# An attention layer and a feed-forward layer on one core: another order of attention steps within a pair of heads, for the first eight pairs

## The chip, the cores and the metric

The kernel runs on one core of a Trainium2 chip. The metric is the device time of one execution in microseconds (us). Five engines take part, each with a queue of its own that it works off in order: TensorE (PE, with its weight loads as PEld), VectorE (DVE), ScalarE (ACT), GpSimd (POOL), and SyncE (SP), which here only issues DMA transfers.

## The reference

A block-causal softmax attention over 8 batches of 8 heads (576 positions, head size 64), followed by a two-layer MLP with the activation h * sigmoid(1.702 h) on the 4608 rows.

```python
scores = scale * np.matmul(q, k.transpose(0, 1, 3, 2))
scores = np.where(block_i >= block_j, scores, -1e9)      # blocks of 64
scores = scores - np.max(scores, axis=-1, keepdims=True)
attn = np.exp(scores); attn = attn / (np.sum(attn, axis=-1, keepdims=True) + 1e-09)
x = np.matmul(attn, v)          # per head; then heads side by side: [4608, 512]
h = x @ w_in                    # w_in  [512, 2048]
g = h * (1.0 / (1.0 + np.exp(-1.702 * h)))
out = g @ w_out                 # w_out [2048, 512]
```

## The kernel before

Two heads form a pair; there are 32 pairs, four to a batch. The queries of a head are cut into five chunks: chunk 0 has 64 queries, chunks 1 to 4 have 128 each, and chunk i sees 64(2i+1) keys. One loop runs over the pairs n. In each turn `step(n)` calls a list of items, in the order that a string of `ORDER` gives for the phase of n: the first string for pairs 0 to 3, the second for 4 to 7, the third from pair 8 on (with `HANDOVER` in place of it for pair 8). The items are:

- a group of chunk numbers, as `1+0` or `2/3`, is `score(n, ...)`: PE multiplies queries and keys into PSUM banks, two heads at a time (a slash starts new banks); `weigh` then lets DVE read each bank, add the mask and take the maximum (line 349), and ACT take the exponential with the sum (line 356); `normalise` prepares the reciprocal on DVE (lines 366 and 369) and lets POOL scale the weights (line 374).
- `a`, `B` and `C` are `flip(...)`: PE turns the scaled weights with the identity (line 101), for chunks 0 and 1 of pair n (`a`), 2 and 3 of pair n-1 (`B`), 4 of pair n-1 (`C`); ACT copies each bank to SBUF (lines 409 and 422).
- `V` is `av(n - 1)`: PE multiplies the turned weights of pair n-1 with the values, 60 matmuls; ACT copies the sums into the ring `xr` (lines 448 and 449). Then the values of a later pair are loaded.
- `L` is `prep(n + 1)`: two DVE transpositions (line 295), first the queries, then the keys, from `raw` to `qk` of the next pair. Behind the second one the loads of a later pair's queries and keys are issued on SP (line 277, eight transfers), since `raw` has one buffer (pairs 1 and 3 have one of their own).
- `-` is an empty place.

The weights of the chunks have one home each (`es[i]`, used again by every early pair), and so has the turned form `pw`. PSUM banks are handed out in rotation by `bank()`: seven of them for pairs 0 to 3, three (`w0` to `w2`) for pairs 4 to 7, where the MLP has the others.

After each item, and after each empty place, two other jobs are advanced up to a quota that is read from the position 2 * (n + (place + 1) / places): `convert`, which turns the 64-bit weights of the MLP into pairs of 32-bit ones, piece by piece (ACT line 218; DVE lines 222, 227, 232; ACT line 241; POOL line 81), and `advance`, which emits MLP matmuls. The MLP works on tiles of 384 rows. Tile 0 can't begin before the attention of pairs 0 to 3 is complete, that is behind the `V` of pair 4; its quota runs from position 8.4 to 17 (`TILES_BY`). So in pairs 0 to 3, and in pair 4 up to its `V`, PE has attention alone, and from there on MLP work lies between the items.

PE's instructions keep the order of the program (`keep_in_program_order`). Those of DVE, ACT, POOL and SP are put in order by the framework's scheduler, by priority (earlier in the program first) and by when it takes an operand to be there. Each engine then works off its queue strictly in that order.

In the steps below 2/3(1) is the scoring of chunks 2 and 3 of pair 1, V(1) the sums of values of pair 1, qk(3) the turned queries and keys of pair 3, and so on.

Of the kernel before, what the change touches and what calls it, by code (L numbers as in the profile page):

```python
# [23 lines left out]


ORDER = (
    "1+0 - B - C - V - 2/3 - L - a - 4 -",
    "1+0 - B - C - V - 2 - 3 L a - 4 - -",
    "3+0/2+1 - - - - V - 4 - - - L -",
)  # L30

# [617 lines left out]
```

## Time and profile before

| what | us |
|---|---|
| three runs, median (lowest to highest) | 1131.25 (1130.1 to 1132.11) |
| the profiled execution, its own time | 1134.02 |
| its span, first to last instruction | 1132.2 |
| PE busy in the span | 1078.8 (95%) |
| DVE, ACT, POOL busy | 586.5, 499.4, 407.1 |
| mean granted TensorE clock | 0.983 of full speed |

The profiled execution is 2.77 us over the median of the runs. Busy time says how long an engine had an instruction in hand; where it was idle, the timeline gives the idle time just before an instruction in square brackets, with what ended it.

### The profile page before, as it was taken

How to read it: one execution, taken by the hardware profiler on the slowest of the kernel's cores; microseconds unless marked ns; L12 is line 12 of the kernel's file. 1: busy time of each engine (PE TensorE's matmuls, PEld its weight loads, DVE VectorE, ACT ScalarE, POOL GpSimd, SP SyncE). 2: the span in 40 equal slices, each digit the busy share in tenths (PEclk: the TensorE clock that was granted, in tenths of full speed). 3: DMA queues.
4: the chain of work that ended last, by engine and by line, in shares of the span. 5: the costliest groups of instructions: out<-in, count | busy, mean ns of one | idle time of the engine just before them, and what ended most of it. 6: DMA issues, size and time to landing. Idle time of an engine off the chain costs nothing. (4 is left out here: it accounts for less than half of the span.)

```text
span 1132.2 us, 20021 instructions
## 1 busy us (share of the span) xinstructions
PE 1078.8 (95%) x6960; PEld 914.1 (81%) x6960; DVE 586.5 (52%) x1856; ACT 499.4 (44%) x1321; POOL 407.1 (36%) x509
## 2 busy tenths in 40 slices
PE   4779999999999999999999999999999999999998
PEld 3567777788788888888888888888888888899997
DVE  5577777554555655654545645555555555211211
ACT  5675777533433533443433434443443443322322
POOL 4455566333333323333333333333333333222222
PEclk8878999999999999999999999999999999999999
DMA  8642642133433243243343243343343332200000
GB/s 176 176 112 58 194 107 70 45 80 84 102 85 81 67 104 66 60 113 85 78 108 82 65 96 63 72 113 78 81 101 73 70 91 50 54 28 1 28 1 29
DMA packets 219366, 91.26 MB, mean 81 GB/s; under 512 B 197760, under 2 KB 197760, under 8 KB 219264
## 3 DMA queue, kind: packets, MB, share of 16 engines
q1 hardware_dynamic: 214528, 89.38, 33.6%
q8 instruction: 55, 0.90, 0.4%
q10 hardware_dynamic: 4736, 0.59, 0.3%
q14 instruction: 47, 0.39, 0.1%
HBM read 45.09 MB, written 9.44 MB: 48 GB/s over the span
## 5 line engine op out<-in xcount | busy, mean ns | idle before, releaser
L81 POOL TENSOR_TENSOR gl<-g,gh 128x384 fp32r<-128x384 f32 x192 | 194.9, 1015 | 528.8 <-ACT gh L561 433.6
L98 PE MATMUL hp<-xh,wih 128*128 128x384 f32 x768 | 265.4, 346 | 11.6 <-DVE g L553 10.5
L553 DVE SCALAR_TENSOR_TENSOR g<-g,hp 128x384 f32<-128x384 f32 x192 | 105.5, 550 | 324.1 <-ACT g L552 322.9
L98 PE MATMUL hp<-xh,wil 128*128 128x384 f32 x768 | 259.1, 337 | 0.0
L98 PE MATMUL hp<-xl,wih 128*128 128x384 f32 x768 | 253.7, 338 | 0.4 <-DVE xl L81 0.4
L552 ACT ACTIVATE g<-hp 128x384 f32<-128x384 f32 x192 | 94.3, 491 | 340.0 <-PE hp L98 337.8
L98 PE MATMUL acc<-woh,gh 128*128 128x512 f32 x576 | 232.2, 403 | 0.0
L98 PE MATMUL acc<-wol,gh 128*128 128x512 f32 x576 | 227.9, 396 | 0.0
L98 PE MATMUL acc<-woh,gl 128*128 128x512 f32 x576 | 227.3, 395 | 0.5 <-POOL gl L81 0.5
L98 PEld LDWEIGHTS hp<-xh,wih 128*128 128x128 f32 x768 | 144.7, 188 | 36.8 <-DVE g L553 21.5
L561 ACT CAST gh<-g 128x384 fp32r<-128x384 f32 x192 | 98.5, 513 | 149.8 <-DVE g L553 149.7
L356 ACT ACTIVATE e<-e,mx 64x64 f32<-64x64 f32 (+4 forms) x240 | 132.3, 552 | 63.7 <-DVE mx L349 63.7
L374 POOL TENSOR_TENSOR e<-e,sm 64x64 f32<-64x64 f32 (+1 forms) x192 | 114.1, 614 | 108.3 <-DVE sm L369 61.5
L98 PEld LDWEIGHTS hp<-xh,wil 128*128 128x128 f32 x768 | 144.8, 189 | 6.8 <-issue 0.2
L98 PEld LDWEIGHTS hp<-xl,wih 128*128 128x128 f32 x768 | 144.1, 188 | 0.7 <-DVE xl L81 0.7
L98 PE MATMUL bank<-qk 64*128 64x320 f32 (+4 forms) x768 | 119.8, 429 | 21.6 <-DVE qk L295 20.4
L98 PEld LDWEIGHTS acc<-woh,gh 128*128 128x128 f32 x576 | 108.2, 188 | 31.8 <-issue 12.0
L98 PEld LDWEIGHTS acc<-wol,gh 128*128 128x128 f32 x576 | 108.1, 188 | 23.5
L98 PEld LDWEIGHTS acc<-woh,gl 128*128 128x128 f32 x576 | 108.3, 188 | 16.7 <-POOL gl L81 1.1
L98 PEld LDWEIGHTS bank<-qk 64*128 64x128 f32 x768 | 68.7, 196 | 62.7 <-issue 26.2
L383 DVE STREAM_TRANSPOSE turned<-e 128x384 f32<-128x384 f32 (+1 forms) x192 | 92.5, 500 | 48.1 <-POOL e L374 48.0
L349 DVE CUSTOM_DVE_ANT_0 e<-bank,mask 64x64 f32<-64x64 f32 (+4 forms) x240 | 88.3, 417 | 29.8 <-PE bank L98 26.2
(50 smaller groups left out, 968.1 us busy)
## 6 DMA issues: line engine op xcount, KB each, us to landing
turned<-turned SPq DMA_DIRECT2D x192, 80.0 KB, 2.1
turned<-turned SPq DMA_DIRECT2D x96, 112.0 KB, 2.2
raw<-in_q_dram SPq DMA_DIRECT2D x128, 72.0 KB, 2.4
out_dram<-osb SPq DMA_DIRECT2D x36, 256.0 KB, 2.2
raw<-in_k_dram SPq DMA_DIRECT2D x120, 72.0 KB, 2.4
turned<-turned SPq DMA_DIRECT2D x96, 88.0 KB, 2.1
words<-in_moe_w_in_dram SPq DMA_DIRECT2D x16, 512.0 KB, 5.6
vp<-in_v_dram SPq DMA_DIRECT2D x60, 128.0 KB, 2.3
```

The source lines that it names most:

```text
L81: eng.tensor_tensor(out=out, in0=in0, in1=in1, op=ALU.subtract)
L98: return tc.keep_in_program_order(nc.tensor.matmul(**kw))
L349: nc.vector.tensor_tensor_reduce(out=e[0:m, hd, lo:hi], in0=s, in1=mk, op0=ALU.add, op1=ALU.min, scale=-0.125, scalar=3e38 if lo == 0 else ...
L356: nc.scalar.activation(out=e[0:m, hd], in_=e[0:m, hd], func=AF.Exp, scale=-1.0, bias=mx[0:m, i, hd : hd + 1], accum_out=sm[0:m, i, hd : hd ...
L374: nc.gpsimd.tensor_tensor(out=x, in0=x, in1=sc.to_broadcast([m, width(i)]), op=ALU.mult)
L383: nc.vector.transpose(out=tw[:, :, SLOT[i] : SLOT[i] + i, hd].rearrange("p b j c -> p j b c"), in_=e[:, hd, 0 : i * P],)
L552: nc.scalar.activation(out=g, in_=hp[:, 0:tt], func=AF.Tanh, scale=1.702)
L553: nc.vector.scalar_tensor_tensor(out=g, in0=g, scalar=1.0, in1=hp[:, 0:tt], op0=ALU.add, op1=ALU.mult)
L561: nc.scalar.copy(out=gh, in_=g)
```

## The change

Two strings are replaced. In pairs 0 to 3 the places go from 16 to 14, in pairs 4 to 7 from 17 to 16. In both, chunks 2 and 3 (of this pair) and `L` come ahead of `V`, and in pairs 0 to 3 chunk 4 does too; `a` comes last but for an empty place, or last but for chunk 4. In pairs 4 to 7 chunk 4 stays behind `V` and `a`. The sum of items is the same, and so are all instructions.

```diff
 ORDER = (
-    "1+0 - B - C - V - 2/3 - L - a - 4 -",
-    "1+0 - B - C - V - 2 - 3 L a - 4 - -",
+    "1+0 - B 2/3 - L C - 4 - V - a -",
+    "1+0 - B - 2 - C - 3 L V - a - 4 -",
     "3+0/2+1 - - - - V - 4 - - - L -",
 )
```

## Rows read from the trace of the kernel before

**Rows 1.** The page's part 2, busy tenths of PE in 40 slices of 28.3 us.

```profile
...
PE   4779999999999999999999999999999999999998
...
```

**Rows 2.** Windows by stage: length; busy us of PE, PEld, DVE, ACT, POOL; clock; DMA.

```profile
...
0.00:86.00 86.00, 55.90 (x465) 43.76 (x466) 53.33 (x186) 52.65 (x156) 41.95 (x65) 0.82 0.64 158
86.00:232.00 146.00, 135.91 (x883) 108.09 (x884) 103.43 (x290) 92.53 (x239) 80.48 (x87) 0.98 0.35 92
232.00:1132.00 900.00, 886.99 (x5617) 762.25 (x5613) 429.72 (x1384) 354.23 (x927) 284.71 (x357) 1.00 0.31 71
...
```

**Rows 3.** Waits of PE, 0 to 86 us: us in total, times, longest.

```profile
...
PE bank L98 <- DVE qk L295: 20.4, 4, 7.2
PE bank L101 <- POOL turned L374: 7.3, 4, 3.9
...
```

**Rows 4.** Timeline of PE: start, us, operation, [idle before it, what ended that].

```profile
...
15.03 1.79 PE L101 MATMUL bank<-ident,turned 128*128 128x128 f32 x6 [3.88 <-POOL turned L374]
...
24.91 0.33 PE L101 MATMUL bank<-ident,turned 128*128 128x128 f32 x1 [2.15 <-POOL turned L374]
...
32.99 1.56 PE L98 MATMUL bank<-qk 64*128 64x320 f32 x8
...
35.29 1.24 PE L98 MATMUL bank<-qk 64*128 64x256 f32 x8
39.30 1.33 PE L98 MATMUL bank<-qk 64*128 64x192 f32 x8 [2.77 <-DVE qk L295]
...
44.24 2.98 PE L98 MATMUL bank<-turned,vx 128*64 128x128 f32 x60
...
48.64 0.87 PE L101 MATMUL bank<-ident,turned 128*128 128x128 f32 x6
...
55.76 1.33 PE L98 MATMUL bank<-qk 64*128 64x192 f32 x8 [5.07 <-DVE qk L295]
...
62.34 2.21 PE L98 MATMUL bank<-turned,vp 128*64 128x64 f32 x44 [0.36 <-ACT turned L422]
...
74.19 1.33 PE L98 MATMUL bank<-qk 64*128 64x192 f32 x8 [5.44 <-DVE qk L295]
...
85.78 0.44 PE L98 MATMUL hp<-xh,wih 128*128 128x384 f32 x1
...
```

**Rows 5.** Timeline of DVE, the same columns, 18 to 55 us.

```profile
...
18.01 0.42 DVE L349 CUSTOM_DVE_ANT_0 turned<-bank,mask 128x256 f32<-128x256 f32 x1 [1.88 <-PE bank L98]
...
26.19 0.78 DVE L295 STREAM_TRANSPOSE qk<-raw 128x576 f32<-128x576 f32 x1
33.83 0.49 DVE L349 CUSTOM_DVE_ANT_0 turned<-bank,mask 128x320 f32<-128x320 f32 x1 [6.86 <-PE bank L98]
...
38.48 0.77 DVE L295 STREAM_TRANSPOSE qk<-raw 128x576 f32<-128x576 f32 x1
...
54.92 0.78 DVE L295 STREAM_TRANSPOSE qk<-raw 128x576 f32<-128x576 f32 x1
...
```

**Rows 6.** Timeline of POOL, around the scaling of chunk 3 of pair 0.

```profile
...
19.67 1.83 POOL L374 TENSOR_TENSOR turned<-turned,sm 128x448 f32<-128x448 f32 x2 [2.00 <-DVE sm L369]
...
```

**Rows 7.** Timeline of PE in pairs 5 and 6, where MLP work lies between.

```profile
...
114.74 0.62 PE L101 MATMUL bank<-ident,turned 128*64 128x128 f32 x4 [1.41 <-ACT turned L409]
...
142.32 1.28 PE L101 MATMUL bank<-ident,turned 128*128 128x128 f32 x10 [1.13 <-DVE mx L349]
...
```

**Rows 8.** Lines of DVE, 0 to 86 us: busy, mean ns, idle before.

```profile
...
L222 DVE TENSOR_SCALAR wm<-wm 128x512 uint32<-128x512 uint32 x9 | 6.2, 693 | 6.7 <-ACT wm L218 6.7
...
```

**Rows 9.** Source line 366, 0 to 86 us: duration ns min/median/max, first and last start.

```profile
...
L366 DVE TENSOR_SCALAR sm<-sm x22: 118/170/947, 13.0 to 79.9; 128x2 f32<-128x2 f32 x17, 64x2 f32<-64x2 f32 x5
...
```

**Rows 10.** Windows, the columns of rows 2: tile 0 begins; DVE at its busiest.

```profile
...
90.00:98.00 8.00, 7.14 (x22) 5.70 (x23) 3.95 (x9) 3.58 (x8) 4.01 (x4) 0.57 0.00 0
160.00:170.00 10.00, 9.90 (x55) 7.78 (x54) 8.26 (x31) 7.69 (x20) 6.35 (x7) 1.00 0.57 125
...
```

**Rows 11.** Timeline of SP's queue: the loads that the second transposition sets off.

```profile
...
39.27 1.96 SPq L277 DMA_DIRECT2D raw<-in_q_dram  x4
...
```

## The prediction

> **What bounds the kernel now.** I read the slices of the page first, then the windows of three stages, the waits of PE in the first stage, and last the timelines there. The slices show PE at 9 tenths nearly everywhere but in the first three [rows 1]. By the windows PE is busy 887.0 of 900 us behind 232 us and 135.9 of 146 us between 86 and 232 us, but 55.9 of the first 86 us; no other engine reaches 72% of any stage [rows 2]. So the end is set by PE, and whatever PE loses before tile 0 of the MLP begins, at 85.78 us [rows 4], moves the end one for one: behind it PE has always something to do. The first stage is where the change acts, and there PE idles 30.1 us: 20.4 us in four waits for qk, 7.3 us in four waits for weights that POOL scales [rows 3], the rest in small ones. The first qk wait, 7.2 us, is the first load; the change can't touch it. That leaves 13.3 us, which the timeline shows ahead of 1+0 of pairs 2, 3 and 4: 2.77, 5.07 and 5.44 us [rows 4]. No transfer causes them. DVE turned the queries of pair 2 at 26.19 us, then stood idle 6.86 us for the scores of chunk 2 of pair 1, and turned the keys only at 38.48 us, behind the weighing of chunks 2 to 4 of pair 1 [rows 5]. The scores it waited for stood behind V(0) on PE. DVE waits for PE and then PE for DVE, in turn: that is the loop that the change cuts.
>
> **The change part by part.** No instruction is added or removed; only places are.
>
> *Pairs 0 to 3, the qk waits.* Now, between the last score of chunk 4 of pair n and 1+0 of pair n+1, PE has nothing (2.77 to 5.44 us, above). Afterwards V(n-1) and a(n) stand there, 2.98 and 0.87 us at full clock [rows 4], 3.85 us together. DVE's way from the scores of chunk 4 to the turned keys stays as it is, since `L` was ahead of chunk 4 before too, and yet the keys come out behind chunk 4's weighing; I take that the scheduler puts them there again. Then the gaps shrink by 2.77, 3.85 and 3.85: 10.5 us. Bounds: if the keys are now turned ahead of chunk 4, all of 13.3 us; if one merge of a weight piece (three DVE instructions of 0.69 us [rows 8], 2.1 us) gets in ahead of them in each pair, 10.5 - 3 x 2.1 = 4.2 us. I take 10.5, since rows 5 show the order itself.
>
> *Pair 0, the waits for scaled weights.* a(0) waits 3.88 us for POOL [rows 4]. Chunk 4 of pair 0 now comes behind a(0) and goes ahead of it: its 1.24 us (by the same item of pair 1 [rows 4]) fill part of that wait. DVE stood 1.88 us for just these scores [rows 5], and POOL's scaling of chunk 3 started 2.00 us late on a reciprocal queued behind them [rows 6]; with that gone the two short waits in B(0), 1.3 us of the 7.3 less 3.88 and 2.15, go too. The 2.15 us wait in C(0) [rows 4] gets chunks 2 and 3 of pair 1 ahead of it, 1.56 us [rows 4]. Together 1.24 + 1.3 + 1.56 = 4.1 us; bounds 0 (POOL is what is late) and 7.3 (all POOL waits). I take 4.1, as each part has a row.
>
> *V moved behind chunk 4: queues.* V(n-1) needs ACT's copies of the turned chunk 4. On ACT these may now stand behind the exponentials of chunks 2 and 3, while only chunk 4's scores lie between C and V on PE. The nearest row is a V that waited 0.36 us for such a copy [rows 4]; three times that is 1.1 us. Bounds 0 and 3 x 1.41 = 4.2 us, the longest wait for a copy [rows 7]. On SP the transfers of a later pair's queries and keys, the four for the queries taking 1.96 us to issue [rows 11], now come ahead of the values instead of behind them. They wait for the second transposition, and the values queue behind them for that long; who needs the values is the V a whole pair on, over 13 us. I cost this at nothing; without that cover it would be 4 us or so a pair, two such groups of transfers. `prep` moved ahead of C on DVE only puts 1.5 us where DVE stood idle [rows 5].
>
> *Pair 4 up to V(3).* Tile 0 waits for V(3), and there 2(4) and 3(4) now come ahead of it, with three banks and no MLP work between. Their own PE time isn't lost: it is work that need not be done later. But three changes of bank owner (2 to C, C to 3, 3 to V) stand uncovered. Each costs between nothing and 1.41 us, the waits of such kind that show [rows 7]; I take 1.2, near the two rows, as nothing covers them: 3.6 us, bounds 0 and 4.2.
>
> *Pairs 5 to 7.* There MLP work lies between all items. Two changes from scores to another owner (2 to C, 3 to V) stand in place of one (3 to `a`). I take 0.5 us a pair, 1.5 us; bounds 0 and 3 x 1.13 = 3.4 [rows 7]. Below zero would be possible by the wider space between scoring and B or C, which ends waits such as those for POOL; only a small one is there to end, so I add none. The rest of the MLP quota is tied to positions and comes out even by position 17.
>
> *The clock* is taken as unchanged. In 90 to 98 us it was granted at 0.57 of full speed, most of it at 1.2 instead of 2.4 GHz, after the idle stretches before [rows 10]. If such a stretch goes, PE gains about half of its 7.1 busy us there, 3.5 us; if one more comes, it loses as much. That is a bound on both sides.
>
> *The sum:* 10.5 + 4.1 - 1.1 - 3.6 - 1.5 = 8.4 us less. From the profiled execution, 1134.0 us, that makes 1125.6; the median of the runs is 2.8 us below it, and from 1131.25 it makes 1122.8, which is the forecast. A cross-check on DVE: it is busy 53.3 us in the first 86 [rows 2], 5.7 of which pass before its first input, and would have some 4 us more to do before V(3), for chunks 2 and 3 of pair 4 and one more `prep`. With tile 0 beginning at about 77 us (85.8 - 14.6 + 1.1 + 3.6, and near 2 us for the scores done early) DVE is busy 57 of 72 us, 0.80. Its busiest ten microseconds with MLP work beside it show 0.83 [rows 10]. It fits, with little room.
>
> **The rivals.**
>
> *The keys come first and the clock holds.* All 13.3 us of qk waits and all 7.3 us of POOL waits go, and 3.5 us of clock come back, less 2.5 us for banks: 21.6 us, 1109.7. For it: DVE's 6.86 us of idling [rows 5] is pure slack. Against it: POOL's scaling does take its time.
>
> *DVE becomes the bound of the first stage.* Its idle time goes, but in-order queues leave it no more than the 0.66 of now (53.3 of 80.3 us [rows 2]) to 0.75. At 0.75 tile 0 begins at 5.7 + 57/0.75 = 82 us, and less 2 us for the scores done early this is 5.8 us ahead of now; less 1.5 in pairs 5 to 7, 4.3 us, and 1127; at 0.70 tile 0 would begin at 87 us and nothing is left, 1131. For it: one sort of DVE instruction, the small scaling of sums, takes 118 ns at least, 170 in the median and 947 at most [rows 9], so DVE's work grows when it meets something. Against it: merges of weight pieces can slip behind tile 0's start, 2.1 us each.
> The Trainium skill (SBUF — State Buffer, section "Who interferes with whom") says that certain DVE instructions and GpSimd's exclude each other on a shared port pair, the later one standing still until the earlier is done; that speaks against packing the two closer. The 947 ns agree with it. If all 22 of those instructions took 947 ns, DVE would have some 13 us more, and this rival would hold.
>
> *Slower: three banks.* In pair 4 the three uncovered changes of owner, and in pairs 5 to 7 two each, make nine. If DVE reads a bank only behind a merge instruction it has already begun, each costs 1.41 + 0.69 = 2.1 us [rows 7, 8], 18.9 us in all, against 14.6 - 1.1 = 13.5 us gained: 5.4 us slower, 1136.7. It decides from 1.5 us for each of the nine. For it: these waits exist with four-place gaps now. Against it: in pairs 5 to 7 MLP matmuls stand between, and PE is idle 10.1 of 146 us there now for all reasons together [rows 2].
>
> *It doesn't do what it says.* The scheduler's order of DVE stays the old one, V goes into gaps that reopen elsewhere, and the time stays within 2 us of 1131.
>
> **How the numbers follow.** The forecast (5 to 14 us less) 0.50; keys first and clock 0.17; DVE-bound 0.16; three banks 0.12; no effect 0.05. A measurement of this kernel tells 0.2%, 2.3 us, from no change. Half of the DVE case is within that, most of the last too: faster 0.75, same 0.13, slower 0.12. The range goes from 1109, the second case, to 1131, the poor end of the DVE case; left out are the slower case and a bit beyond.
>
> **What would show it.** Right: the waits of PE for qk in the first stage fall from 20.4 to about 10 us; V(1) and V(2) stand behind chunk 4 with PE idle at most 2 us ahead of 1+0 of the next pair; DVE's 6.86 us idle ahead of 2/3(1) is gone; tile 0 begins at 75 to 78 us; PE's waits between there and pair 8 are no more than 5 us over now. Wrong: qk waits of the old size (the keys still later in DVE's queue), DVE over 0.85 with PE waiting for it (the second rival), or PE waits on banks in pairs 4 to 7 of over 13 us (the third).

## The result, and the profile after

The changed kernel is a little slower: 1134.1 us in the median of 20 runs (1129.4 to 1136.7) against 1130.9 us (1129.4 to 1132.7) for the kernel before, a ratio of 1.0026 with a 95% interval of 1.0017 to 1.0034. The forecast was 1122.8 us, with 1109 to 1131 as its range.

The profiled execution of the changed kernel took 1131.2 us, 3 us under that median, at a mean granted clock of 0.988; the runs of 1134 us and over have 0.980 to 0.985. So the traces below show an execution with less low clock than the usual one, and where the rest of it lies in an execution of 1134 us was not seen.

The windows of the three stages of the changed kernel, with the columns of [rows 2]:

```profile
...
0.00:86.00 86.00, 58.20 (x487) 42.22 (x488) 63.85 (x209) 58.73 (x173) 48.88 (x72) 0.90 0.65 157
86.00:232.00 146.00, 135.99 (x877) 109.09 (x876) 96.37 (x276) 87.61 (x231) 74.96 (x84) 0.97 0.37 96
232.00:1132.00 900.00, 884.10 (x5600) 759.91 (x5598) 427.44 (x1372) 351.76 (x918) 284.55 (x355) 1.00 0.31 71
...
```

Where [rows 2] had 55.90 us of PE in the first 86 us it has 58.20 now, DVE has 63.85 instead of 53.33, and in the two later stages PE's busy time is as it was to within 3 us. PE's waits in the first 86 us, as in [rows 3]:

```profile
...
PE bank L98 <- DVE qk L295: 11.0, 4, 7.1
PE bank L98 <- ACT xr L449: 4.7, 1, 4.7
PE bank L101 <- POOL turned L374: 3.8, 3, 2.9
PE bank L98 <- ACT turned L409: 1.9, 2, 1.6
PE bank L101 <- ACT turned L409: 1.6, 2, 1.4
...
```

The waits for qk fell from 20.4 to 11.0 us, those for POOL from 7.3 to 3.8. New is one wait of 4.7 us for ACT's copy of sums of values, and waits for its copies of turned weights are 3.5 us in sum instead of 0.6. PE's timeline shows where, in the columns of [rows 4]:

```profile
...
14.54 1.23 PE L101 MATMUL bank<-ident,turned 128*128 128x128 f32 x6 [2.91 <-POOL turned L374]
...
31.00 0.76 PE L98 MATMUL bank<-qk 64*128 64x192 f32 x8 [0.59 <-DVE qk L295]
...
42.27 0.76 PE L98 MATMUL bank<-qk 64*128 64x192 f32 x8 [0.78 <-DVE qk L295]
...
51.24 2.99 PE L98 MATMUL bank<-turned,vp 128*64 128x128 f32 x60
...
57.55 0.69 PE L98 MATMUL bank<-qk 64*128 64x192 f32 x2 [2.52 <-DVE qk L295]
62.93 1.32 PE L98 MATMUL bank<-qk 64*128 64x192 f32 x6 [4.69 <-ACT xr L449]
...
75.84 2.98 PE L98 MATMUL bank<-turned,vx 128*64 128x128 f32 x60 [0.32 <-ACT turned L422]
...
81.16 0.44 PE L98 MATMUL hp<-xh,wih 128*128 128x384 f32 x1 [1.10 <-ACT xh L495]
...
83.44 0.44 PE L98 MATMUL hp<-xl,wih 128*128 128x384 f32 x1 [1.10 <-DVE xl L81]
...
```

For three pairs the change does what was forecast, and more. 1+0 of pair 2 stands at 31.00 instead of 39.30 us, that of pair 3 at 42.27 instead of 55.76: 13.5 us ahead. From there the lead shrinks. The first bank of 1+0 of pair 4 is filled at 57.55, the next one only at 62.93, 11.3 us ahead of 74.19. V(3) begins at 75.84, and tile 0's first matmul follows at 78.75 instead of 85.78: 7.0 us ahead, or 8.9 with the scores of chunks 2 and 3 of pair 4, 1.8 us at full clock (rows below), that are already done. Tile 0's last matmul of the first layer stands 2.9 us ahead, at 203.51 instead of 206.43, and that is what is left at the end of the span, 1129.4 instead of 1132.2 us. So 4.6 us are lost in the passage from pair 3 to tile 0, and 6 us more while tile 0 runs.

### The profile page after: what moved, and what is told of

Same layout as the page of the kernel before. It is cut to its first block, busy times and chain, and to the rows that moved or that the text cites. A ratio compares the mean times of both kernels' runs of the same rounds, so it can differ in the third digit from the quotient of the medians.

```text
span 1129.4 us, 20023 instructions
## 1 busy us (share of the span) xinstructions
PE 1078.3 (95%) x6960; PEld 911.2 (81%) x6960; DVE 587.7 (52%) x1856; ACT 498.1 (44%) x1321; POOL 408.4 (36%) x509
## 5 line engine op out<-in xcount | busy, mean ns | idle before, releaser
L98 PE MATMUL bank<-qk 64*128 64x320 f32 (+4 forms) x768 | 122.9, 424 | 18.5 <-DVE qk L295 11.0
L98 PEld LDWEIGHTS acc<-woh,gh 128*128 128x128 f32 x576 | 108.8, 189 | 30.9 <-issue 10.7
```

The costliest lines, as they stand in the source:

```text
L98: return tc.keep_in_program_order(nc.tensor.matmul(**kw))
```

## The experiments

The ratios are to the kernel before on the same chip, with 95% intervals; the first line repeats the result.

| run | pairs 0 to 3 | pairs 4 to 7 | median us | ratio |
|---|---|---|---|---|
| changed kernel | new | new, 16 places | 1134.1 | 1.0026 (1.0017 to 1.0034) |
| ctl_after | new | new, 16 places | 1134.2 | 1.0032 (1.0018 to 1.0047) |
| p1_only | old | new, 16 places | 1137.9 | 1.0067 (1.0054 to 1.0079) |
| p0_only | new | old, 17 places | 1122.1 | 0.9921 (0.9909 to 0.9934) |
| places16 | new | old, 16 places | 1123.7 | 0.9940 (0.9922 to 0.9958) |
| places18 | new | old, 18 places | 1124.0 | 0.9943 (0.9926 to 0.9959) |
| two_first | new | old, but chunk 2 ahead of C, 17 | 1123.5 | 0.9934 (0.9919 to 0.9948) |
| places17 | new | new, 17 places | 1128.2 | 0.9975 (0.9963 to 0.9987) |
| pair4_old | new | pair 4 old, 5 to 7 new, 17 | 1122.2 | 0.9921 (0.9907 to 0.9935) |
| banks7 | new | new, 16, seven banks in pair 4 | 1123.3 | 0.9937 (0.9924 to 0.9951) |
| p0_banks7 | new | old, 17, seven banks in pair 4 | 1122.9 | 0.9925 (0.9910 to 0.9939) |
| p0_late | new | old, 17, weight pieces later | 1139.2 | 1.0075 (1.0060 to 1.0090) |
| after_late | new | new, 16, weight pieces later | 1139.8 | 1.0078 (1.0060 to 1.0095) |

### The two strings apart

p0_only takes the first string alone, p1_only the second alone.

```diff
     "1+0 - B 2/3 - L C - 4 - V - a -",
-    "1+0 - B - 2 - C - 3 L V - a - 4 -",
+    "1+0 - B - C - V - 2 - 3 L a - 4 - -",
```

> Only the first string is changed: pairs 0 to 3 in the new order, pairs 4 to 7 in the old one. Theory A (the new order of pairs 4 to 7 gives the gain back: in the trace of the changed kernel the stretch from tile 0's first matmul to its last is 131.9 us long against 127.8, and pair 4 takes 14.6 us from the end of its first scores to the end of V(3)): 1+0 of pair 4 begins some 11 us earlier than in the kernel before, tile 0 some 10 us earlier, and the time is 1120 to 1125 us. Theory B (the gain is lost at the passage from pair 3 to pair 4, where the number of banks drops from seven to three and ACT's copies of V(2) stand behind weight pieces, whatever the order behind it): the lead at tile 0 is 6 us or less, the time 1126 to 1131.

```diff
-    "1+0 - B 2/3 - L C - 4 - V - a -",
+    "1+0 - B - C - V - 2/3 - L - a - 4 -",
     "1+0 - B - 2 - C - 3 L V - a - 4 -",
```

> Only the second string is changed: pairs 0 to 3 in the old order, pairs 4 to 7 in the new one. Theory A (the new order of pairs 4 to 7 costs 8 to 12 us by itself): slower, 1137 to 1143 us, with tile 0 beginning 3 to 6 us later than before and the stretch of tile 0 some 4 us longer. Theory B (pairs 4 to 7 in the new order cost little; the loss comes from the passage that the new order of pairs 0 to 3 makes): 1130 to 1135 us.

The first string alone saves 8.9 us (0.9921 of 1130.9), the second alone costs 7.6. On top of the first, the second costs 12 us. The time of p0_only is the one of theory A; that of p1_only lies at its lower edge, while its tile 0 begins only some 2.5 us later than before and is 129.3 us long against 127.8, both less than theory A said. So the change holds two opposite effects.

### The control

> The changed kernel once more, unchanged, for a second profile: its first profile has a time of 1131.2 us and a clock of 0.988, while most of its 20 runs lie at 1133.5 to 1135 us with clocks of 0.982 to 0.983. If what differs is where the low clock falls, this profile shows 10 us or more additional low clock at the same instructions order, and idle time that is the same within 1 us; if what differs is waits, the idle time of PE differs by 3 us.

Neither: the second profile has the same clock as the first, 0.988, and a span equal to 0.1 us, so it tells nothing about the runs at 1134 us.

### What in the second string costs

Three kernels take steps from the old second string to the new one, on top of the new first string; a fourth, further down, keeps the old order in pair 4 alone.

```diff
 # two_first
+    "1+0 - B - 2 - C - V - 3 L a - 4 - -",
 # places16
+    "1+0 - B - C - V - 2 - 3 L a - 4 -",
 # places17
+    "1+0 - B - 2 - C - 3 L V - a - 4 - -",
```

> Pairs 0 to 3 in the new order; in pairs 4 to 7 chunk 2 alone is moved ahead of C, and chunk 3, L, V, a and 4 stand as in the old order with 17 places. The run with only the first string changed has 1122.1 us, the changed kernel 1134.2, so the new second string costs 12 us. Theory C (what costs is V behind chunk 3, which sets tile 0 back and puts its opening beside chunk 3's weighing and scaling): 1120 to 1124 us here. Theory D (what costs is a bank hand-over from chunk 2 to C without enough between): 1125 to 1130.

> Pairs 0 to 3 in the new order; in pairs 4 to 7 the old order with one empty place less at the end, 16 places. Theory E (the lost place costs): 1127 to 1133 us, with waits for ACT's copies ahead of the last transposes of B and for POOL in pair 8. Theory C: 1120 to 1124 us, as with 17 places.

> The changed kernel with one more empty place at the end of the second string, 17 as before, so that chunk 4 keeps two quotas of MLP work behind it ahead of the next pair's scores and, in pair 8, of B and C. Theory E (what costs is the lost place: ACT's exponentials of chunk 4 meet B's copies of the next pair, waits of 2.2, 1.1 and 1.1 us and the low clock behind them): 1122 to 1127 us. Theory C (V behind chunk 3): 1131 to 1135 us.

Chunk 2 ahead of C costs little: 0.9934 instead of 0.9921, 1.5 us, and the intervals overlap. So do those of one place less in the old order (0.9940, 2.1 us); with one place more, places18 below, the ratio is 0.9943, so these 2.1 us are not shown to be the price of the place. Chunk 3 and L ahead of V with 17 places give 0.9975, 4.6 us over two_first, and the place taken away on top of that 5.8 us more. D fell. places17 lies between the ranges of C and E, and places16 in that of C: each names a part at most, and the lost place costs only together with the new order.

The kernels with 16 and 17 places in the new order differ in the waits of PE late in tile 0, in the same places of the program. First the changed kernel, then places17:

```profile
...
166.92 0.89 PE L101 MATMUL bank<-ident,turned 128*64 128x128 f32 x4 [2.20 <-ACT turned L409]
...
193.80 0.63 PE L101 MATMUL bank<-ident,turned 128*64 128x128 f32 x4 [1.06 <-ACT turned L409]
...
197.02 1.20 PE L101 MATMUL bank<-ident,turned 128*128 128x128 f32 x9 [1.10 <-POOL turned L374]
...
```

```profile
...
162.69 0.63 PE L101 MATMUL bank<-ident,turned 128*64 128x128 f32 x4 [1.20 <-ACT turned L409]
...
189.81 0.63 PE L101 MATMUL bank<-ident,turned 128*64 128x128 f32 x4 [0.82 <-ACT turned L409]
...
192.62 1.20 PE L101 MATMUL bank<-ident,turned 128*128 128x128 f32 x9 [0.68 <-POOL turned L374]
...
```

The first row of each is the end of B of pair 6, which needs a bank that ACT has to copy first; the other two are the end of B and then C of pair 7, in pair 8's turn. With a place less the three waits are 4.4 us in sum instead of 2.7. The clock differs too. Windows of the tile's whole stretch and of 18 us around that first wait, for the changed kernel and then for places17, in the columns of [rows 2]:

```profile
...
78.75:210.62 131.87, 118.77 (x788) 94.98 (x784) 91.46 (x248) 82.59 (x216) 73.90 (x79) 0.96 0.35 91
84.00:92.00 8.00, 6.84 (x27) 6.44 (x28) 4.94 (x8) 3.71 (x7) 3.36 (x4) 0.79 0.00 0
154.00:172.00 18.00, 14.97 (x65) 10.66 (x62) 11.71 (x36) 9.97 (x28) 10.39 (x12) 0.81 0.18 52
...
```

```profile
...
81.09:206.20 125.11, 115.61 (x787) 92.48 (x784) 89.73 (x248) 82.69 (x216) 73.72 (x79) 0.99 0.36 96
84.00:93.00 9.00, 6.71 (x26) 5.78 (x26) 6.66 (x12) 3.15 (x6) 3.68 (x3) 0.81 0.00 0
150.00:168.00 18.00, 16.73 (x94) 13.04 (x93) 15.31 (x44) 12.68 (x35) 11.14 (x13) 1.00 0.24 70
...
```

Of the changed kernel's 131.87 us PE is idle for 13.1, in places17 for 9.5 of 125.11. So of the 6.8 us between them 3.6 are idle time and 3.2 busy time, which goes with the lower clock. Around the wait of 2.20 us the clock was granted at 0.81, some of it at 1.2 GHz; at the same items in places17, with a wait of 1.20, it stayed at 1.00. That the longer wait brings the fall is not shown, and places16 speaks against it. There the same wait, at the end of B of pair 6, is longer still, and the clock stays at 1.00:

```profile
...
160.55 0.62 PE L101 MATMUL bank<-ident,turned 128*64 128x128 f32 x4 [2.52 <-ACT turned L409]
...
150.00:168.00 18.00, 15.24 (x121) 12.65 (x120) 15.28 (x40) 12.32 (x33) 12.48 (x15) 1.00 0.15 42
...
```

What joins the lost place to the lower clock therefore stays open.

Now V behind chunk 3. Pair 4 was given back its old order, and pairs 5 to 7 kept the new one with 17 places:

```diff
+        if n == HP:
+            return "1+0 - B - C - V - 2 - 3 L a - 4 - -".split()
```

> Pairs 0 to 3 in the new order, pair 4 in the old one, pairs 5 to 7 in the new one with 17 places. With pairs 4 to 7 all in the new order and 17 places the ratio to the kernel before was 0.9975, with all of them in the old one 0.9921, some 6 us apart. Theory I (those 6 us are lost in pair 4 alone, where tile 0's opening meets the scaling of chunk 3 on POOL: DVE's subtractions took 1151 ns in the median there and 552 in the old order, and PE waited for ACT and DVE at the first matmuls): ratio 0.991 to 0.994, 1121 to 1124 us, subtractions at 550 ns. Theory J (they are lost in pairs 5 to 7): ratio 0.996 to 0.999, 1127 to 1130 us, with the subtractions at 550 ns all the same.

0.9921, the ratio of p0_only: of the two theories the place is that of theory I. The 6 us are lost in pair 4, and in pairs 5 to 7 the new order with 17 places costs nothing that can be measured. Theory I's reason is another matter. It points at DVE's subtractions that split tile 0 (x minus its rounded part), by source line 81 with durations as min, median and max, in p0_only, places17 and pair4_old:

```profile
...
L81 DVE TENSOR_TENSOR xl<-xr,xh x4: 551/552/560, 76.9 to 78.3; 128x384 fp32r<-128x384 f32 x4
...
```

```profile
...
L81 DVE TENSOR_TENSOR xl<-xr,xh x4: 539/1155/1290, 81.3 to 84.8; 128x384 fp32r<-128x384 f32 x4
...
```

```profile
...
L81 DVE TENSOR_TENSOR xl<-xr,xh x4: 551/553/560, 77.1 to 78.5; 128x384 fp32r<-128x384 f32 x4
...
```

They take 1155 ns in the median where chunk 3 stands ahead of V and 552 where it doesn't. In the changed kernel the median is 1151, in p1_only 1154, in two_first 546, in places16 550, in the kernel before 554. POOL's timeline tells what runs beside them; the changed kernel:

```profile
...
79.01 2.42 POOL L374 TENSOR_TENSOR turned<-turned,sm 128x448 f32<-128x448 f32 x2 [1.24 <-DVE sm L369]
...
```

POOL scales chunk 3 of pair 4 just then, and takes 2.42 us for what took 1.83 in [rows 6]. In the old order that scaling comes after tile 0 is opened. PE's waits at tile 0's first matmuls, in places17:

```profile
...
83.75 0.44 PE L98 MATMUL hp<-xh,wih 128*128 128x384 f32 x1 [1.35 <-ACT xh L495]
...
85.90 0.44 PE L98 MATMUL hp<-xl,wih 128*128 128x384 f32 x1 [1.01 <-DVE xl L81]
...
```

In pair4_old and p0_only neither wait is there. The first is not the subtractions' doing, since the kernel before, with 554 ns, waits for the same cast:

```profile
...
88.19 0.45 PE L98 MATMUL hp<-xh,wih 128*128 128x384 f32 x1 [1.09 <-ACT xh L495]
...
```

That leaves 1.0 us that PE waits for the subtractions themselves, of about 6.

More is lost on the scores of chunks 2 and 3 that were moved ahead of V. In pair4_old they come behind the opening of tile 0, in places17 ahead of it, in a stretch whose clock was granted at 0.53. First pair4_old, with the window of its tile 0, then places17:

```profile
...
83.78 0.81 PE L98 MATMUL bank<-qk 64*128 64x320 f32 x4
86.11 1.02 PE L98 MATMUL bank<-qk 64*128 64x448 f32 x4
...
76.96:201.44 124.48, 115.62 (x796) 91.47 (x793) 92.04 (x259) 85.24 (x224) 74.28 (x81) 1.00 0.35 92
...
```

```profile
...
71.56 2.26 PE L98 MATMUL bank<-qk 64*128 64x320 f32 x4
76.08 2.14 PE L98 MATMUL bank<-qk 64*128 64x448 f32 x4
...
60.00:78.00 18.00, 11.80 (x40) 7.43 (x40) 10.46 (x30) 11.82 (x34) 8.60 (x11) 0.53 0.64 167
...
```

The same scores take 4.40 us instead of 1.83. places17 begins tile 0 4.1 us later than pair4_old, 2.3 more than the work done early is worth at full clock, and the slower scores, by 2.6 us, account for that. Of the tile's stretch, 125.11 us against 124.48 with 1.8 us less to do, another 2.5 are lost: 0.6 in idle time (9.5 us against 8.9), and the rest goes with the stretch at 0.81, from 84 to 93 us. That the waits at the opening bring this fall of the clock is not shown either: p0_banks7 below, with the old second string and subtractions of 544 ns in the median, was granted 0.66 from 80 to 85 us.

### The passage from pair 3 to pair 4

The wait of 4.7 us for the copy of V(2) is also in p0_only, with 4.4. ACT's timeline in the changed kernel:

```profile
...
56.78 0.62 ACT L241 CAST woh<-wm 128x512 fp32r<-128x512 f32 x1 [1.81 <-DVE wm L232]
57.30 0.63 ACT L218 ACTIVATE wm<-words 128x512 f32<-128x512 f32 x1
61.22 0.62 ACT L241 CAST woh<-wm 128x512 fp32r<-128x512 f32 x1 [3.29 <-DVE wm L232]
61.74 0.62 ACT L218 ACTIVATE wm<-words 128x512 f32<-128x512 f32 x1
62.30 0.58 ACT L449 COPY xr<-bank 128x512 f32<-128x512 f32 x1
...
```

V(2) was done on PE at 54.2 us. Its copy (line 449) stands in ACT's queue behind two weight pieces, and the second cast (line 241) waits for DVE's merge, which waits for POOL:

```profile
...
60.49 0.69 DVE L232 SCALAR_TENSOR_TENSOR wm<-words,wm 128x512 uint32<-128x512 uint32 x1 [1.10 <-POOL wol L81]
...
```

Two runs take away what lets PE feel that: the fall from seven banks to three in pair 4, where 1+0 gets the bank that V(2) is still in.

```diff
-        if turns["n"] < HP:
+        if turns["n"] < HP or (turns["n"] == HP and not done["split"]):
```

> The changed kernel, in which pair 4 keeps seven banks until tile 0 begins, so that its first scores need not wait for the bank that holds V(2). Theory B (the drop to three banks at pair 4 gives back 5 us and more, and the low clock behind it as much again): the wait of PE for ACT's copy of V(2), 4.7 us, goes, tile 0 begins 5 to 9 us earlier than in the changed kernel, and the time is 1124 to 1129 us. Theory A (what is lost is lost behind tile 0's beginning): tile 0 begins earlier and the time stays at 1131 to 1135.

> Only the first string changed, and seven banks kept in pair 4 until tile 0 begins. In the run with only the first string changed PE waits 4.4 us ahead of 1+0 of pair 4 for ACT's copy of V(2), because the banks drop to three. In the changed kernel the seven banks took tile 0's beginning from 78.8 to 76.2 us and the time from 1134.2 to 1123.3. If the seven banks are worth the same here: 1111 to 1116 us. If the copy of V(2) is waited for in any case a little later (PE then waits for the turned B of pair 3 or for V(3)): 1118 to 1122.

In p0_banks7 it gains nothing (0.9925 against 0.9921). The timeline of banks7 shows why:

```profile
...
58.42 0.76 PE L98 MATMUL bank<-qk 64*128 64x192 f32 x8 [2.52 <-DVE qk L295]
...
63.89 2.37 PE L101 MATMUL bank<-ident,turned 128*128 128x128 f32 x10 [4.12 <-ACT xr L448]
...
```

The scores pass, and the transposes right behind them wait 4.12 us for the copies of V(2) all the same: by the rotation of seven, B's banks for chunk 3 of pair 3 are the two that V(2) filled. So more banks only move the wait to the next item, as the second arm for p0_banks7 has it. All the same banks7 is 10.7 us faster than the changed kernel (0.9937 against 1.0032): theory A falls, and theory B's gain came, if not its path, since tile 0 begins only 2.5 us earlier. That changes the reading of the second string. With seven banks in pair 4 the new second string with 16 places is level with the old one with 17 (0.9937 against 0.9925, the intervals overlap), though DVE's subtractions are slow as before (1018 ns). So neither these nor the lost place cost anything that can be measured there: the 12 us need the three banks of pair 4. Of the two scores of chunks 2 and 3, banks7 has the second at full speed again:

```profile
...
67.06 1.51 PE L98 MATMUL bank<-qk 64*128 64x320 f32 x4 [0.80 <-ACT turned L422]
...
70.63 1.02 PE L98 MATMUL bank<-qk 64*128 64x448 f32 x4
...
```

They take 2.53 us, against 4.05 in the changed kernel. The stretch of tile 0 is 126.1 us long instead of 131.9; of these 5.8 us 3.1 are idle time (10.0 us against 13.1) and 2.7 busy time. Why the three banks bring them stays open.

Two more runs take the weight pieces out of the passage, by having fewer of them due by pair 4.

```diff
-WEIGHTS_BY = ((0, 0), (8, 13), (14.5, 32))
+WEIGHTS_BY = ((0, 0), (6, 3), (8, 8), (14.5, 32))
```

> Only the first string changed, and the weight pieces due later (8 instead of 13 by pair 4), so that in ACT's queue no piece stands between the exponentials of chunk 4 of pair 3 and the copies of V(2). Theory F (the wait of 4.4 us ahead of 1+0 of pair 4 comes from two weight pieces ahead of these copies): that wait falls under 1 us, tile 0 begins 4 to 8 us earlier than at 76.8, the time is 1112 to 1119 us. Rival G (the copies are late for another reason, or tile 0 then waits for its weights, which are now converted beside the MLP): tile 0 begins within 2 us of 76.8 or waits appear behind it for the pieces, 1120 to 1126 us.

> The changed kernel with the weight pieces due later, as in the other run. Theory F (pieces ahead of the copies of V(2), and DVE and POOL busy with pieces in pair 4): PE's wait for the copy goes, the low clock behind it shortens, tile 0 begins 4 to 8 us earlier than at 78.8 us, the time is 1122 to 1129 us. Rival H (what the second string costs lies in the end of each pair, the place lost): tile 0 begins earlier, and 3 us at most is left of that in the time, 1130 to 1134 us.

The first half of theory F is right: the wait for the copy is gone, and PE gets tile 0 open at 68.65 us, 8.1 us earlier than p0_only. The second half is wrong, and rival G's second arm is right by far more than it said: the time is 17 us more than p0_only's. Waits of PE in p0_late from 75 us on, and the window of its tile 0:

```profile
...
PE hp L98 <- POOL wil L81: 4.5, 5, 1.4
...
PE hp L98 <- ACT wih L241: 3.3, 4, 1.1
...
PE acc L98 <- POOL wol L81: 2.1, 1, 2.1
...
```

```profile
...
68.65:217.55 148.90, 126.87 (x796) 96.61 (x793) 100.73 (x272) 90.79 (x233) 79.45 (x85) 0.92 0.38 108
...
```

PE now waits for pieces over and over, 9.9 us by these rows, and the clock over the whole stretch is 0.92. Tile 0 takes 148.9 us instead of 123.1. after_late shows the same (148.0 us, 12.4 us of waits for the first layer's pieces), and its time lies above the ranges of both its theories.

### More room at the end of a pair

```diff
-    "1+0 - B - 2 - C - 3 L V - a - 4 -",
+    "1+0 - B - C - V - 2 - 3 L a - 4 - - -",
```

> Only the first string changed, and the second, old one with one empty place more at its end, 18 places. One place less cost 2.1 us in the old order (1123.7 against 1122.1, by ratios 0.9940 and 0.9921) and 6 us in the new one. If the distance from chunk 4 to the next pair's B is what counts and it isn't long enough yet: 1118 to 1121 us. If 17 places are enough: 1121 to 1124.

17 places are enough: 18 give 0.9943, no better than 0.9921, with overlapping intervals.

The fastest of all these is the new order in pairs 0 to 3 with the old one in pairs 4 to 7 (p0_only, level with pair4_old): 1122.1 us, 0.9921 of the kernel before.

## Why the prediction was right or wrong

The sum failed in two places. Its terms for the first string make 13.5 us (10.5 + 4.1 - 1.1), and p0_only saves 8.9; a wait of 4.4 us for ACT's copy of V(2), which no step had, is about the difference. Its terms for the second string make 5.1 us (3.6 + 1.5), and that string costs 12 on top of the first. There the step on pair 4 failed, with its premise that PE's time for the early scores "isn't lost": at the clock granted there they took 4.05 us for 1.83.

*The qk waits (10.5 us forecast): right.* They fell by 9.4 us. What is left ahead of 1+0 of pairs 2, 3 and 4 is 0.59, 0.78 and 2.52 us, where the step left 0, 1.2 and 1.6. The keys come out behind chunk 4's weighing, as it took them to, and DVE's idle time of 6.86 us [rows 5] is gone.

*Pair 0, the scaled weights (4.1 us): right in sum.* The POOL waits fell by 3.5 us. The parts differ: a(0) waits 2.91 instead of 3.88 us, the two short waits in B(0), which were to go, stay at 0.35 and 0.56, and C(0)'s 2.15 is gone whole.

*V moved behind chunk 4 (1.1 us): of the right size, and the bigger wait was missed.* V waited 1.6 us once and 0.3 once for a copy. But the step looked only at who V waits for, and not at who waits for V. V(2) now ends next to 1+0 of pair 4, its copy stands on ACT behind two weight pieces, and 1+0 of pair 4 waits 4.7 us for it. That row has no counterpart in the kernel before, where all of chunks 2 to 4 and a qk wait lay between V and the next pair.

*Pair 4 up to V(3) (3.6 us): the mechanism was wrong.* At the three changes of bank owner PE waits at most 0.3 us in the changed kernel. What was put at nothing is what costs: the scores of chunks 2 and 3, moved into a stretch of low clock, took 2.2 us more than at full clock, and in places17 2.6. With what follows in tile 0, pair 4's new order costs about 6 us by the medians of places17 and pair4_old, and 4.5 by their profiles. The waits for tile 0's `split`, which comes right behind V(3) and was in no step, are 1.0 us of it for the slow subtractions. banks7 shows that all this needs the three banks; by which path it does is open.

*Pairs 5 to 7 (1.5 us): wrong.* With 17 places they cost nothing (pair4_old). The place taken away costs 5.8 us in the new order, and nothing clear of noise in the old one, or with seven banks in pair 4. No run has pair 4 in the old order and pairs 5 to 7 in the new one with 16 places, so in which pairs these 5.8 us arise is not shown. The sentence that the quota comes out even by position 17 left out that 3.6 us of idle time and a lower clock can come with it.

*The clock (taken as unchanged, bounds 3.5 us either way): wrong.* It was low where the moved scores ran, and within tile 0 the windows of the changed kernel show two more stretches below 1.00 (0.79 at 84 to 92 us, 0.81 at 154 to 172), where the kernel before had one [rows 10] and pair4_old has none.

*Where the sum came out, luck had a part.* By the traces tile 0's lead of 8.9 us is near the 9.9 that the terms up to there make (10.5 + 4.1 - 1.1 - 3.6), but the 4.7 us wait for V(2)'s copy stands where 3.6 for changes of bank owner were forecast. Behind the opening 1.5 us were forecast to be lost, and 6 were. (The prediction's own terms put tile 0's beginning at 77.9 us, not at about 77; it is at 78.75.)

*"Whatever PE loses before tile 0 begins moves the end one for one": wrong as a rule.* p0_late begins tile 0 17 us earlier than the kernel before and takes 8 us more. Tile 0 uses up weight pieces, and these are made by ACT, DVE and POOL at their own pace; a lead at the opening counts only as far as pieces are ready.

Of the rivals, the slower one had the sign and nearly the size (5.4 us slower forecast, 3.2 measured). Its path is not the one seen, since waits at its nine changes of bank owner are not what costs, but its condition is: with seven banks in pair 4 instead of three the loss is gone.

## What to carry to other kernels

A step that is moved has two sides: list who waits for its results and in which queue these results leave, not only what it waits for. Where one order changes in two phases, cost them apart, and cost the passage between them as a phase of its own; here one half was worth 8.9 us, the other cost 12, and the fastest kernel is the half. Work that is done early is not done for nothing: it runs at the clock that is granted there, here half. An earlier start of a bound stage is a gain only if what that stage consumes is ready earlier too.

## What the runs showed of the hardware

DVE's subtraction of two SBUF tiles took 552 ns in the median with POOL idle (p0_only), and 1151 in the changed kernel beside two POOL multiplications, which took 2.42 instead of 1.83 us, and a POOL subtraction. The Trainium skill (SBUF — State Buffer, section "Who interferes with whom") says that a DVE instruction with two SBUF inputs and a GpSimd instruction that reads SBUF exclude each other; the traces agree that both get slower; that the later one stands still for the whole of the earlier one can't be told from these rows. The prediction had the rule, and weighed it for other instructions.

The same scores took 1.83 us on PE at a granted clock of 1.00 and 4.40 where it was granted at 0.53. A long wait and a fall of the clock don't go together in every case here: around waits of 2.20 and 2.52 us at the same items the clock was 0.81 in the one kernel and 1.00 in the other.

The changed kernel took 1129.4 to 1136.7 us in 20 runs, the fastest at a mean granted clock of 0.989 and those over 1134.1 at 0.982 or 0.983. Single profiles of two such kernels mislead by 6 us here: in the profiles the changed kernel is 2.8 us ahead, in the medians 3.2 behind.
